# A cached attention block: warm-up matmuls of 80 columns, branch hints moved forward, the last product in two halves

## The chip, the core and the metric

The kernel runs on one core of a Trainium2 chip. The metric is the device time of one execution in microseconds. A profile is one further execution, recorded by the hardware profiler; its times count from the first instruction of the program.

## The reference

```python
B, Sq, D = 8, 112, 640
H, Sk, Dh = 32, 512, 192
q = (x @ wq).reshape(B, Sq, H, Dh).transpose(0, 2, 1, 3)
scores = einsum("bhqd,bhkd->bhqk", q, k_cache) * (Dh ** -0.5)
p = softmax(scores, axis=-1)
o = einsum("bhqk,bhkd->bhqd", p, v_cache)
return o.transpose(0, 2, 1, 3).reshape(B, Sq, H * Dh) @ wo
```

All tensors are bf16. The caches hold 8 x 32 x 512 x 192 elements each, some 50 MB, and are read once.

## The kernel before

`build_main` does the work. A second program, `build_mha_kernel`, stands behind it in the same instruction stream and runs only if a flag is raised: `build_main` counts softmax sums out of a safe range, and if there are none, every engine jumps over the second program to the end.

The work is cut into 64 units, `NU = 64`; a unit is four heads of one batch element, and eight units of the same heads make a group (`NG = 8`). Of a unit TensorE computes the scores (`do_S`, line 922, 96 matmuls on 32-row tiles), the product with V (`do_PV`, line 943, 16 matmuls) and the transposes of its result (`do_T`, line 954). Between these lie slots, (i, 0) and (i, 1) for step i, which a table fills with "pairs" (`do_pair`, lines 846 and 903): a `Q` pair is one 128-column slice of the next group's query product, an `O` pair one 128-row block of the output product with `wo`. Each pair has two halves, h = 0 and 1, in two PSUM banks, 6 and 7. `bank_free` makes a half wait until the bank's former content has been copied out.

`held` (line 846) is a matmul without a weight load of its own: it uses the weights that are in the array. In a pair, step q loads the weights once by `pe.matmul` for h = 0 and uses them again by `held` for h = 1.

The other engines: VectorE transposes K (`do_KT`, line 1080), reduces the softmax sums (`do_NM`), and copies the halves of an `O` pair out (`do_OE`, line 1104), adding the sum so far. ScalarE computes the exponentials (line 1021) and copies query slices and transposes. GpSimd reorders `wq` and the middle heads of V and keeps the count for the flag. SP issues every DMA in one fixed list (`loads`, line 1285; per unit four pieces of K and four of V, with a wait for the buffer to be free) and then the seven stores of the output (line 1288), each after VectorE's two copies of that block.

**Start.** TensorE first waits for the identity matrix, then runs the warm-up at lines 958 to 962: one matmul of the identity with 240 columns and `WARM = 30` further `held` ones, all into PSUM bank 7, results unused. Then come the transposes of the first four blocks of x (`do_X`, line 842, five per block; a block waits for its piece of x), and the query product of group 0 for the first half of the rows (`do_Q0(c, 0)`, line 869, 120 matmuls on 32-column tiles, four at a time). It waits for the copies of the transposes by VectorE (line 1109) and ScalarE (line 997) and for five pieces of `wq`. The last three blocks of x, the scores of unit 0 and the second half of the query product follow.

**End.** Slot (65, 1) holds the last `O` pair, group 7, block 6. Its two halves are copied out by VectorE and stored by SP.

**Jump.** `get_flag` (line 830) loads the flag into a register of each engine; behind the block's own barrier every engine runs a compare-and-branch (line 1309) to `main_end`. `mark_branch_hint_location` puts a branch-prefetch hint for that jump into an engine's stream at the place where it is called: for TensorE at i = 65 (line 978), ScalarE at the end of i = 64 (1066), VectorE after its loop (1138), GpSimd after unit 63 (1211), SP before the last store (1290).

Of the kernel before, what the change touches and what calls it, by code (L numbers as in the profile page):

```python
# [666 lines left out]
def build_main(nc, x, k_cache, v_cache, wq, wo, out, flag, regs, hints):  # L667
# [4 lines left out]
    NU = NG * B  # L672
    DC = D // 128
    R = B * SQ
    MT = R // 128
# [7 lines left out]
    RW = DH + 2  # L683
    FULL, FRONT, BACK = range(3)
    FILL = {(24, 0): 5, (24, 1): 6, (48, 0): 4, (48, 1): 5, **{(i, j): 2 for i in range(56, 64) for j in range(2)}}
    WARM = 30
    NM = 2
    KP = [4] * NU
# [67 lines left out]
    with ExitStack() as es:  # L756
        def sb(name, shape, dt):
            return es.enter_context(nc.sbuf_tensor(name, shape, dt))
# [27 lines left out]
        ident = sb("ident", [128, 128], BF16)  # L786
        dmy = sb("dmy", [128, 2], F32)
        ps = es.enter_context(nc.psum_tensor("ps", [128, 8, 512], F32))
# [46 lines left out]
        def _(pe):  # L835
# [37 lines left out]
            def do_pair(i, j):  # L873
                if slot[i, j] is None:
                    return
                (k, g, c), part = slot[i, j]
                pair = (k, g, c)
                if k == "Q":
                    if c == 0:
                        W(pe, gW, DC * g)  # L880
                    n, width, inc = DC, HQ, pQ
                else:
                    if part != BACK and 8 * g + last_unit(c) + 1 > min(i - 2 + j, NU - 2):
                        W(pe, aT, 8 * g + last_unit(c) + 1)
                    n, width, inc = 6, HO, pO
                steps = {FULL: range(n), FRONT: range(n // 2), BACK: range(n // 2, n)}[part]
                fill = FILL.get((i, j), 1)
                for q in steps:
                    if k == "Q":
                        w = wqs[:, g % 2, q, 128 * c:128 * (c + 1)]  # L890
                        rhs = [xT[:, q, HQ * h:HQ * (h + 1)] for h in range(2)]
                    else:
                        if c == 0 and q % 2 == 0:
                            W(pe, mWO[g % 2][q // 2], 32 * (g // 2 + 1))
                        w = oT[:, q, 128 * c:128 * (c + 1)]
                        rhs = [wos[:, g % 2, q, HO * h:HO * (h + 1)] for h in range(2)]
                    for h in range(2):
                        if q == 0:
                            bank_free(pe, pair, h)
                        cuts = fill if q else 1  # L900
                        for f in range(cuts):
                            cs = slice(width * f // cuts, width * (f + 1) // cuts)
                            mm = (held if h or f else pe.matmul)(ps[:, 6 + h, cs], w, rhs[h][:, cs], q == 0,  # L903
                                                                 q == n - 1 and f == cuts - 1)
                        if q == n - 1:
                            mm.then_inc(inc, 1)

# [48 lines left out]

            W(pe, gI, 1)
            W(pe, vI, 1)
            warm = ident[:, None, 0:60].broadcast_to([128, 4, 60])
            pe.matmul(ps[:, 7, 0:240], ident[:], warm, start=True, stop=True)  # L960
            for j in range(WARM):
                held(ps[:, 7, 0:240], ident[:], warm, True, True)
            for m in range(4):
                do_X(m)
            for c in range(6):
# [24 lines left out]
        @block.scalar  # L990
        def _(act):
            W(act, vI, 1)
            act.activation(dmy[:, 1:2], dmy[:, 0:1], ACTF.Exp)

            def evac_x(m):
                W(act, pXT, m + 1)
                act.activation(xT[:, :, 128 * m:128 * (m + 1)],
                               psb[:, m, 0:D].rearrange("p (c s) -> p c s", c=DC), ACTF.Copy).then_inc(aX, 1)

            def evac(g, c, h):  # L1000
                n = q_index[g, c, h]
                W(act, pQ, n + 1)
                if g >= 2 and c == 0 and h == 0:
                    W(act, pS, 4 * B * (g - 1))
                act.activation(qT[g % 2][:, c, HQ * h:HQ * (h + 1)], ps[:, 6 + (n % 2 if g == 0 else h), 0:HQ],  # L1005
                               ACTF.Copy).then_inc(aQ, 1)

            def evac_pair(i, j):
                if slot[i, j] and slot[i, j][0][0] == "Q" and slot[i, j][1] != FRONT:
                    for h in range(2):  # L1010
                        evac(*slot[i, j][0][1:], h)

            def exp(u, a):
                W(act, pS, 4 * u + a + 1)
                if a == 3 and u >= 2:
                    W(act, gM, u + 1)
                if a == 0:
                    W(act, pPV, u - 1)
                    if u < 2:
                        W(act, gV, 1)  # L1020
                act.activation(pT[u % 2][:, a, :, 0:SQ], ps[:, a, 0:4 * SQ].rearrange("p (t q) -> p t q", t=4), ACTF.Exp,  # L1021
                               scale=scale).then_inc(aEX, 1)

            def norm(u):
                W(act, vRC, u + 1)
                W(act, pT_, u - 1)
                for e in range(2):
                    ins = act.activation(os_[u % 2][:, DH * (2 + e):DH * (3 + e)], pv_of(u)[0:SQ, 1, e, 1:1 + DH], ACTF.Copy,  # L1028
                                         scale=rinv[:, u % 4, 2 + e:3 + e])
                ins.then_inc(aNM, 1)  # L1030

            def tevac(u):
                g, b = divmod(u, B)
                W(act, pT_, u + 1)
                if g > 0:
                    W(act, pO, 2 * (MT * (g - 1) + (SQ * b + SQ - 1) // 128 + 1))
                src = psb[:, bank_of_T(u), 2:2 + 4 * RW].rearrange("p (k w) -> p k w", k=2)[:, :, 0:3 * SQ]
                act.activation(oT[:, :, SQ * b:SQ * (b + 1)].rearrange("p (k c) q -> p k c q", k=2),  # L1038
                               src.rearrange("p k (c q) -> p k c q", c=3), ACTF.Copy).then_inc(aT, 1)

            for m in (1, 3):
                evac_x(m)
            for c in range(6):
                evac(0, c, 0)
            for m in (4, 5):
                evac_x(m)
            for c in range(6):
                if c < 4:
                    exp(0, c)
                evac(0, c, 1)  # L1050
            for i in range(1, NU + 2):
                if i < NU:
                    exp(i, 0)
                if i >= 2:
                    tevac(i - 2)
                if i < NU:
                    exp(i, 1)
                evac_pair(i, 0)
                if i < NU:
                    exp(i, 2)  # L1060
                    exp(i, 3)
                if 1 <= i <= NU:
                    norm(i - 1)
                evac_pair(i, 1)
                if i == NU:
                    hints[mybir.EngineType.Activation] = act.mark_branch_hint_location()
            get_flag(act)

        @block.vector
        def _(dve):  # L1070
# [52 lines left out]
                        do_OE(*slot[i, j][0][1:], h)  # L1123

            for i in range(NU + 1):
                kts = [divmod(n, 4) for n in range(*kt_ahead[i])]
                for it in kts[:3]:
                    do_KT(*it)
                if i < NU:
                    do_OEs(i, 0)  # L1130
                if i >= 1:
                    do_NM(i - 1)
                if i == NU:
                    do_OEs(i, 0)
                do_OEs(i, 1)
                for it in kts[3:]:
                    do_KT(*it)
            hints[mybir.EngineType.DVE] = dve.mark_branch_hint_location()
            W(dve, gC, NU + 1)
            dve.tensor_reduce(tot[:], cnt[:], axis=mybir.AxisListType.XY, op=ALU.add).then_inc(vT, 1)  # L1140
            W(dve, vT, 1)
# [8 lines left out]
        def _(gp):  # L1150
# [48 lines left out]
            for u in range(NU):  # L1199
# [7 lines left out]
                gp.wait_ge(gC, u + 2)  # L1207
                if u + NM < NU:
                    middle(u + NM)
                if u == NU - 1:  # L1210
                    hints[mybir.EngineType.Pool] = gp.mark_branch_hint_location()
            get_flag(gp)

# [1 line left out]
        def _(sp):  # L1215
            loads = []
# [52 lines left out]
            for u in range(4, NU + 1):  # L1269
# [8 lines left out]
                for g in range(1, NG):  # L1278
                    d = u - (8 * g - 1)
                    if 0 <= d < 3:  # L1280
                        load_wo(g, d)
            for dst, src, s, count, waits in loads:
                for ws, wv in waits:
                    W(sp, ws, wv)
                sp.dma_start(dst, src).then_inc(s, 16)
            for m in range(MT):
                W(sp, vO, 2 * (MT * (NG - 1) + m + 1))
                sp.dma_start(out.rearrange("b s d -> (b s) d")[128 * m:128 * (m + 1)], ob[:, m, :]).then_inc(mOUT[m], 16)
                if m == MT - 2:
                    hints[mybir.EngineType.SP] = sp.mark_branch_hint_location()  # L1290
            get_flag(sp)
            for m in range(MT):
                sp.wait_ge(mOUT[m], 16)
# [49 lines left out]
```

## Time and profile before

| | us |
|---|---|
| five timed runs, median | 406.02 |
| lowest and highest of them | 405.08, 407.72 |
| profiled execution, its own time | 404.48 |
| its span, first to last instruction | 399.4 |
| TensorE busy in the span | 390.8 |
| DMA queue busy, share of 16 engines | 90.2% |
| HBM read over the span | 117.54 MB |

The page gives busy time of each engine, the chain of work that ended last (followed back from the last instruction), and groups of like instructions: line, engine, operation, output and input, count, busy time, mean duration, and what ended the idle time before them. A timeline lists instructions in order of time, merged where they are alike: start, duration of the whole group, engine, line. Matmul ends are modelled, so matmuls in a row overlap: the distance of their starts tells what one costs. The span begins and ends with the program's own instructions; the execution's time is longer by what the runtime does before and after them, instruction fetches among it. Those fetches are DMA packets on two queues of the kind "instruction", q8 and q14.

### The profile page before, as it was taken

The numbers are of one execution on the slowest core, as the hardware profiler recorded it, in microseconds if no ns is written. First come the engines' busy times: TensorE is split into PE (matmuls) and PEld (weight loads), VectorE is DVE, ScalarE is ACT, GpSimd is POOL, SyncE is SP. The second block draws the span as 40 slices with busy tenths as digits, with TensorE's granted clock in tenths as the row PEclk, the third lists the DMA queues.
The fourth block names the chain that finished last, engine by engine and source line by source line (L and its number), as shares of the span: only waits on it lengthen the run. The fifth ranks groups of instructions, "written<-read, shape, count | busy, mean of one in ns | idle before, by whom it ended". The sixth has DMA issues, their size and how long they took to land.

```text
span 399.4 us, 20206 instructions
## 1 busy us (share of the span) xinstructions
PE 390.8 (98%) x9073; PEld 242.4 (61%) x8285; DVE 292.9 (73%) x569; ACT 254.3 (64%) x550; POOL 141.3 (35%) x420
## 2 busy tenths in 40 slices
PE   7999999999999999999999999999999999999995
PEld 1656665656656656565666656666565665667661
DVE  1665788786796787876787776886788677789843
ACT  2577665667656766667756676566764766666661
POOL 5522443243442253233352255233344223223320
PEclk9999999999999999999999999999999999999999
DMA  8999999999998999989998999989899979999611
GB/s 271 375 372 341 328 344 336 350 353 332 368 321 268 308 294 344 316 273 317 319 334 288 286 311 337 337 270 311 260 300 321 316 254 324 302 327 300 208 44 59
DMA packets 88443, 120.04 MB, mean 301 GB/s; under 512 B 9760, under 2 KB 88352, under 8 KB 88352
## 3 DMA queue, kind: packets, MB, share of 16 engines
q1 hardware_dynamic: 88352, 118.72, 90.2%
q8 instruction: 69, 1.13, 1.2%
q14 instruction: 22, 0.18, 0.2%
HBM read 117.54 MB, written 1.15 MB: 297 GB/s over the span
## 4 chain that ended last, share of the span: by engine, by line
PE 96%; DVE 2%; issue 1%; DVEq 0%; POOL 0%; POOLq 0%
PE ps L846 24%; PE ps L943 22%; PE ps L922 21%; PE ps L903 20%; PE ps L954 6%; PE ps L869 1%; PE ps L862 1%; DVE kt L1080 1%; DVE xs L1104 0%; PE ps L842 0%; DVE xT L1109 0%; DVE acc L1104 0%; DVEq L830 0%; PE ps L960 0%; POOL ident L1153 0%
## 5 line engine op out<-in xcount | busy, mean ns | idle before, releaser
L1080 DVE STREAM_TRANSPOSE kt<-kr 128x384 int32<-128x384 int32 x256 | 191.5, 866 | 2.4 <-DMA kr<-in_k_cache_dram 2.1
L1021 ACT ACTIVATE pT<-ps 128x448 bf16<-128x448 f32 x256 | 130.4, 560 | 75.6 <-PE ps L922 75.4
L922 PEld LDWEIGHTS ps<-qT,kt 32*128 32x128 bf16 x6144 | 77.3, 93 | 31.0 <-issue 24.3
L943 PE MATMUL ps<-vs,pT 128*128 128x193 bf16 x512 | 95.2, 247 | 0.1
L846 PE MATMUL ps<-wos,oT 128*128 128x320 bf16 (+3 forms) x476 | 93.8, 267 | 0.0
L1203 POOL TENSOR_SCALAR bad<-rinv 112x4 f32<-112x4 f32 x64 | 14.7, 229 | 220.6 <-DVE rinv L1089 220.6
L903 PE MATMUL ps<-wos,oT 128*128 128x320 bf16 x336 | 90.6, 289 | 0.7 <-DVE xs L1104 0.7
L922 PE MATMUL ps<-qT,kt 32*128 32x112 bf16 x6144 | 88.6, 208 | 1.0 <-issue 0.8
L943 PE MATMUL ps<-vm,pT 128*128 128x193 bf16 x512 | 85.1, 247 | 0.3 <-issue 0.3
L846 PE MATMUL ps<-xT,wqs 128*128 128x448 bf16 (+4 forms) x282 | 74.5, 309 | 0.0
L903 PE MATMUL ps<-xT,wqs 128*128 128x448 bf16 (+2 forms) x210 | 72.8, 347 | 0.2 <-DVE acc L1104 0.2
L1028 ACT ACTIVATE os<-ps,rinv 112x192 bf16<-112x192 f32 x128 | 46.9, 417 | 36.2 <-DVE rinv L1089 34.7
L1185 POOL COPY vm<-vs 128x384 int32<-128x384 int32 x128 | 61.4, 510 | 10.6 <-DMA vs<-in_v_cache_dram 3.8
L903 PEld LDWEIGHTS ps<-wos,oT 128*128 128x128 bf16 x336 | 32.7, 97 | 45.5 <-issue 39.7
L943 PEld LDWEIGHTS ps<-vs,pT 128*128 128x128 bf16 x512 | 47.7, 98 | 18.4 <-ACT oT L1038 10.5
L1005 ACT ACTIVATE qT<-ps 128x448 bf16<-128x448 f32 x96 | 48.0, 552 | 16.8 <-PE ps L903 10.8
L1086 DVE TENSOR_REDUCE sm<-ps 112x4 f32<-112x8 f32 x64 | 10.6, 166 | 57.2 <-PE ps L943 57.0
L1104 DVE TENSOR_TENSOR acc<-ps,acc 128x320 f32<-128x320 f32 x84 | 37.0, 481 | 16.5 <-PE ps L903 16.5
L943 PEld LDWEIGHTS ps<-vm,pT 128*128 128x128 bf16 x512 | 46.6, 97 | 3.0 <-issue 0.2
L1038 ACT ACTIVATE oT<-ps 128x672 bf16<-128x672 bf16 x64 | 46.4, 725 | 1.9 <-PE ps L954 1.9
L903 PEld LDWEIGHTS ps<-xT,wqs 128*128 128x128 bf16 x210 | 20.4, 97 | 35.0 <-issue 30.2
L1092 DVE TENSOR_TENSOR os<-ps,rinv 112x384 bf16<-112x384 f32 x64 | 35.7, 558 | 6.5
(42 smaller groups left out, 177.1 us busy)
## 6 DMA issues: line engine op xcount, KB each, us to landing
kr<-in_k_cache_dram SPq DMA_DIRECT2D x256, 192.0 KB, 4.1
vs<-in_v_cache_dram SPq DMA_DIRECT2D x256, 192.0 KB, 4.0
wos<-in_wo_dram SPq DMA_DIRECT2D x48, 160.0 KB, 4.3
wqr<-in_wq_dram SPq DMA_DIRECT2D x35, 192.0 KB, 5.1
out_dram<-xs SPq DMA_DIRECT2D x7, 160.0 KB, 2.5
wqs<-in_wq_dram SPq DMA_DIRECT2D x5, 192.0 KB, 4.2
xs<-in_x_dram SPq DMA_DIRECT2D x2, 320.0 KB, 3.3
xs<-in_x_dram SPq DMA_DIRECT2D x1, 480.0 KB, 5.7
```

The costliest lines, as they stand in the source:

```text
L846: return pe.add_instruction(mybir.InstMatmult(name=nc.get_next_instruction_name(), engine=mybir.EngineType.PE, ins=[pe.lower_ap_or_imm(rhs ...
L903: mm = (held if h or f else pe.matmul)(ps[:, 6 + h, cs], w, rhs[h][:, cs], q == 0, q == n - 1 and f == cuts - 1)
L922: mm = pe.matmul(ps[:, a, SQ * t:SQ * (t + 1)], kt[u % NT][p, t, c // 2, :, c % 2], qT[g % 2][p, c, SQ * b:SQ * (b + 1)], start=(c == 0), ...
L943: mm = pe.matmul(pv[:, k, e, o0:o0 + DH + 1], pT[u % 2][:, a, t, :], src[:, a, v0:v0 + DH + 1], start=(t == 0), stop=(t == 3), skip_group_ ...
L1005: act.activation(qT[g % 2][:, c, HQ * h:HQ * (h + 1)], ps[:, 6 + (n % 2 if g == 0 else h), 0:HQ], ACTF.Copy).then_inc(aQ, 1)
L1021: act.activation(pT[u % 2][:, a, :, 0:SQ], ps[:, a, 0:4 * SQ].rearrange("p (t q) -> p t q", t=4), ACTF.Exp, scale=scale).then_inc(aEX, 1)
L1028: ins = act.activation(os_[u % 2][:, DH * (2 + e):DH * (3 + e)], pv_of(u)[0:SQ, 1, e, 1:1 + DH], ACTF.Copy, scale=rinv[:, u % 4, 2 + e:3 + e])
L1038: act.activation(oT[:, :, SQ * b:SQ * (b + 1)].rearrange("p (k c) q -> p k c q", k=2), src.rearrange("p k (c q) -> p k c q", c=3), ACTF.Co ...
L1080: dve.transpose(dst, src).then_inc(vKT, 1)
L1092: dve.tensor_tensor(os_[u % 2][:, 0:2 * DH].rearrange("p (e d) -> p e d", e=2), pv[0:SQ, 0, :, 1:1 + DH], rinv[:, u % 4, 0:2][:, :, None]. ...
L1104: ins = dve.tensor_tensor(ob[:, m, cs] if g == NG - 1 else acc[:, m, cs], src, acc[:, m, cs], op=ALU.add)
L1185: ins = gp.tensor_copy(vm[u % NM][:, :, (DH + 2) * h:(DH + 2) * h + DH].bitcast(I32), vs[u % NV][:, :, 32 + DH * (1 + h):32 + DH * (2 + h) ...
```

## The change

Three edits.

1. The warm-up matmuls have 80 columns in place of 240; their number is the same.
2. The hints of four engines stand earlier: ScalarE's at the head of i = 55, VectorE's at the head of i = 60, GpSimd's after unit 53, SP's 56 loads ahead of the end of its list. TensorE's stays.
3. In the pair of slot (65, 1) all six steps of half 0 come first, then all six of half 1, which loads its weights anew at each step. Other pairs are unchanged.

```diff
+    HINT_AT = {"act": 55, "dve": 60, "pool": 53, "sp": 56}
...
-                for q in steps:
+                apart = (i, j) == (NU + 1, 1)
+                for q, hs in [(q, [h]) for h in range(2) for q in steps] if apart else [(q, range(2)) for q in steps]:
...
-                    for h in range(2):
+                    for h in hs:
...
-                            mm = (held if h or f else pe.matmul)(ps[:, 6 + h, cs], w, rhs[h][:, cs], q == 0,
-                                                                 q == n - 1 and f == cuts - 1)
+                            mm = (pe.matmul if h == hs[0] and f == 0 else held)(ps[:, 6 + h, cs], w, rhs[h][:, cs], q == 0,
+                                                                               q == n - 1 and f == cuts - 1)
...
-            warm = ident[:, None, 0:60].broadcast_to([128, 4, 60])
-            pe.matmul(ps[:, 7, 0:240], ident[:], warm, start=True, stop=True)
+            warm = ident[:, None, 0:20].broadcast_to([128, 4, 20])
+            pe.matmul(ps[:, 7, 0:80], ident[:], warm, start=True, stop=True)
             for j in range(WARM):
-                held(ps[:, 7, 0:240], ident[:], warm, True, True)
+                held(ps[:, 7, 0:80], ident[:], warm, True, True)
...
             for i in range(1, NU + 2):
+                if i == HINT_AT["act"]:
+                    hints[mybir.EngineType.Activation] = act.mark_branch_hint_location()
...
-                if i == NU:
-                    hints[mybir.EngineType.Activation] = act.mark_branch_hint_location()
...
             for i in range(NU + 1):
+                if i == HINT_AT["dve"]:
+                    hints[mybir.EngineType.DVE] = dve.mark_branch_hint_location()
...
-            hints[mybir.EngineType.DVE] = dve.mark_branch_hint_location()
...
-                if u == NU - 1:
+                if u == HINT_AT["pool"]:
                     hints[mybir.EngineType.Pool] = gp.mark_branch_hint_location()
...
-            for dst, src, s, count, waits in loads:
+            for n, (dst, src, s, count, waits) in enumerate(loads):
+                if n == len(loads) - HINT_AT["sp"]:
+                    hints[mybir.EngineType.SP] = sp.mark_branch_hint_location()
...
-                if m == MT - 2:
-                    hints[mybir.EngineType.SP] = sp.mark_branch_hint_location()
```

## The prediction

> **What bounds the kernel now.** I read the totals and the chain first, then the start and the end in order of time, then what lies behind the span. From the page:
>
> ```profile
> span 399.4 us, 20206 instructions
> PE 390.8 (98%) x9073; PEld 242.4 (61%) x8285; DVE 292.9 (73%) x569; ACT 254.3 (64%) x550; POOL 141.3 (35%) x420
> PE 96%; DVE 2%; issue 1%; DVEq 0%; POOL 0%; POOLq 0%
> ```
>
> TensorE is busy 98% of the span and is 96% of the chain: from its first real work on, one unit follows another without a hole. So the time is the moment at which TensorE starts real work, plus a stream that the diff doesn't touch, plus what follows its last matmul. The start (timeline):
>
> ```profile
> 1.70 6.10 PE L846 MATMUL ps<-ident 128*128 128x240 bf16 x30
> 7.64 1.28 PE L842 MATMUL ps<-ident,xs 128*128 128x128 bf16 x20
> 8.40 1.30 ACT L997 ACTIVATE xT<-ps 128x640 bf16<-128x640 bf16 x2 [6.17 <-PE ps L842]
> 9.80 5.86 PE L869 MATMUL ps<-xT,wqs 128*32 128x448 bf16 x120 [0.88 <-DVE xT L1109]
> ```
>
> The warm-up takes 6.10/30 = 203 ns per 240 columns, half speed; the trace's clock record grants full speed at 7.56 us, just before the first transpose. The data had been there for long (view of the tile xs, time to landing):
>
> ```profile
> DMA to landing us min/median/max: 3.1/3.5/5.7
> ```
>
> The pieces of x are issued at 0.74, 1.24 and 6.04 us and land at 3.83, 4.70 and 11.76. So TensorE computes nothing useful for 3.8 us after x is there. The end (timeline):
>
> ```profile
> 393.60 0.30 PE L903 MATMUL ps<-wos,oT 128*128 128x320 bf16 x1 [0.45 <-DVE xs L1104]
> 395.26 0.30 PE L846 MATMUL ps<-wos,oT 128*128 128x320 bf16 x1
> 395.46 0.89 DVE L1104 TENSOR_TENSOR xs<-ps,acc 128x320 bf16<-128x320 f32 x2 [1.56 <-PE ps L903]
> ```
>
> Both halves of the last product end together at about 395.4, and VectorE then needs 0.89 for the two. The last store is issued at 396.38. Behind the span, the jumps and the instruction fetches (view of line 1309, then DMA queues from 399.5 to 400.5):
>
> ```profile
> L1309 ACTq COMPARE_BRANCH  x1: 68/68/68, 398.8 to 398.8; - x1
> L1309 PEldq COMPARE_BRANCH  x1: 490/490/490, 398.9 to 398.9; - x1
> ```
> ```profile
> q14 instruction: 4, 0.03, 11.0%
> q8 instruction: 1, 0.02, 9.0%
> ```
>
> Four packets of 8192 B start at 399.78 to 399.92, about 0.9 us after four engines jumped. TensorE's 16384 B follow at 400.18. A semaphore that the program doesn't use rises at 399.73, next only at 402.31 and 403.15, then six times by 403.44; some 200 others are reset until 404.0. I read it as the engines' closing barrier: one engine arrives at once, the others are late. The profiled execution took 404.48 us, its span 399.4, so 5.1 lie outside, most of them here. The timed runs' median is 406.02, 1.54 above this execution; I work out a difference on the profile and add it to the median.
>
> [...]
>
> **The change part by part.** *Warm-up* (31 matmuls, 80 columns for 240). At half speed 80 columns take 203 x 80/240 = 68 ns, the whole 2.1 us from 1.53, ending at about 3.7, before x lands at 3.83. The transposes then start at about 3.9 instead of 7.64. They are still at half speed: 20 x 203 x 128/240 = 108 ns make 2.2 us, to 6.1. ScalarE's second copy (0.65 each, 1.30 for two) follows the last of them with some 0.25 of latency and ends at 7.0, so the query product (L869) starts at about 7.1 instead of 9.80; its first weights landed at 5.89, its fifth piece at 7.94, just about when wanted. The early start thus brings 2.7.[...] The product has 30 steps of 195 ns (5.86/30), double when cold, say 373 to 390[...]. I take 0.9[...]; ends -0.8 and +2.5. What is late next: the third piece of x lands at 11.76, the key transposes end at 13.16, V of unit 0 lands at 19.58 and is wanted at 25.73 less the gain. None bites, so the gain runs through to the end; loads later wait for buffers and move with TensorE.
>
> *Last product.* The same 12 matmuls of 135 ns; the second half loads its six weights again (98 ns each, beside the matmuls, as in the value product, where every matmul has its load). The first half ends near 394.6 and its copy (0.49) lies beside the second half, which no longer waits at 393.9 for its bank and ends at about 395.4. One copy follows: 395.9 instead of 396.35. Gain 0.45, ends 0.2 (loads don't hide) and 0.6. The store, its landing 1.8 us later and the jump follow unchanged.
>
> *Hints.* One instruction per engine moves, 45 to 56 ns each, on engines that have idle time in every unit: nothing. Moved past by SP's hint are 56 load issues; it holds none of them back. What may change is the fetch behind the jump. I counted each engine's instructions in the trace against the 8192 B fetches. ScalarE fetches at its instructions 67, 192, 323, 453, 575, 705 (347.65 us)[...] and jumps at 806. VectorE's last entry is 834 (388.14), jump 857; GpSimd's 454 (356.26), jump 502; SP's 595 (366.52), jump 620. The old hints stand at 798, 841, 497 and 611[...]. From 388.2 to the jump no such packet runs, so these hints fetch nothing. The new ones stand at 697, 790, 439 and 549[...]. The trace doesn't show such a hint at work on these four engines. But somebody reached the barrier at 399.73 without a fetch; only TensorE can have, whose hint at 388.40 is followed by an extra 16384 B at 392.08. If all arrive as early, the barrier is through at about 399.73 + 0.4 = 400.1 or 400.2 instead of 403.44: gain 3.2. Ends 0 (the hint does nothing, or one engine still comes last) and 3.4 (all of 402.31 to 403.15 and the wait before).
>
> Sum: -0.9 - 0.45 - 3.2 = -4.6. On the profiled 404.48 that is 399.9, on the median 406.02 - 4.6 = 401.4.
>
> **The rivals.** *Hints without effect*: [...]one engine misses. Then only start and tail count: -1.35, 404.7; with one of the two late arrivals left (402.31), 0.8 more, 403.9. For it: four hints were useless before.[...] *Clock late*: hints work, the start loses 0.8: -2.9, 403.1.[...] *Slower*:[...] Each engine then stalls at its page entry for a miss, 402.31 - 398.92 = 3.4 us, and misses at the jump as before. GpSimd and SP work units ahead and hide it. ScalarE at 347.7 has 75.6/64 = 1.2 us of idle time per unit before its exponentials, so some 2 stay; VectorE at 388.1 stands in the tail with TensorE behind it, some 2.5. That is +4.5 - 1.35 = +3.1, 409.1; it decides once the stalls exceed 3.4 us. Against it: no old hint fetched at once.
>
> **How the numbers follow.** This kernel's measurement can tell about 0.5%, 2.03 us, from no change: faster is below 404.0, slower above 408.1. All hints work and the clock comes in time: 0.66, 401.4, its own range 399.5 (start +2.5, end +3.4) to 403.2. Clock late: 0.06. Hints without or with partial effect: 0.20, of which 0.04 falls below 404.0 and 0.01 on the far side.[...] Faster 0.66 + 0.06 + 0.04 = 0.76; same 0.15; slower 0.09. The range reaches from 399.4 to 404.7, which takes in the middle of the second case and leaves out some 0.2.
>
> **What would show it.** Warm-up over at 3.7, first transpose at 3.9, query product from 7.1 and ending before 15.66 by about 0.9. The last VectorE line as two copies of 0.49 some 0.8 apart, the last store issued about 0.65 after the last matmul's start, not 1.12. No 8192 B packet within 1.2 us of the jumps, those packets instead at 347, 356, 366 and 388 as before; the gap between time and span down from 5.1 to about 1.9. If that gap stays at 5, the hint step is wrong; if ScalarE or VectorE stand still for 3 us at those page entries, the slower rival is right.

## The result, and the profile after

| | before | after |
|---|---|---|
| timed runs, median, us | 406.24 (48 runs) | 403.32 (27 runs) |
| lowest and highest | 403.93, 410.15 | 400.11, 406.40 |
| ratio of after to before | | 0.992, 95% interval 0.9903 to 0.9937 |
| profiled execution, its own time | 404.48 | 401.15 |
| its span | 399.4 | 399.2 |
| outside the span | 5.1 | 1.9 |

The change is faster by 0.8%, about 3.2 us (the medians differ by 2.9). The ratio and the comparisons below leave out two executions that lay over 1.5% above the fastest of their kernel, one of the change (406.40) and one of the kernel before in the runs of e1 to e4 (411.12). Almost nothing of the gain lies in the span. In the page of the changed kernel the totals, the chain and VectorE's costliest group read:

```profile
span 399.2 us, 20213 instructions
PE 89%; DMA 4%; DVE 4%; issue 1%; SPq 1%; DVEq 0%
L1082 DVE STREAM_TRANSPOSE kt<-kr 128x384 int32<-128x384 int32 x256 | 191.7, 867 | 6.5 <-DMA kr<-in_k_cache_dram 6.1
```

TensorE's share of the chain falls from 96% to 89%, and DMA, which was not in it, has 4%. VectorE's K transposes now wait 6.1 us for K's loads; it was 2.1, in the page before:

```profile
L1080 DVE STREAM_TRANSPOSE kt<-kr 128x384 int32<-128x384 int32 x256 | 191.5, 866 | 2.4 <-DMA kr<-in_k_cache_dram 2.1
```

This is the first sign of where the earlier start went.

**The start.** Timeline of the changed kernel (start, duration of the group, engine, line):

```profile
1.58 2.20 PE L847 MATMUL ps<-ident 128*128 128x80 bf16 x30
...
4.30 2.08 PE L843 MATMUL ps<-ident,xs 128*128 128x128 bf16 x20 [0.52 <-DMA xs<-in_x_dram]
...
7.27 1.80 PE L870 MATMUL ps<-xT,wqs 128*32 128x448 bf16 x16 [0.89 <-DMA wqs<-in_wq_dram]
...
9.23 6.79 PE L870 MATMUL ps<-xT,wqs 128*32 128x448 bf16 x104 [0.15 <-DMA wqs<-in_wq_dram]
```

The warm-up ends at 3.78. The first transpose now waits for x (0.52 us), which in this execution landed at 4.26, and the query product waits for each of its weight pieces, which landed at 7.13 to 9.19, 1.2 us later than in the profile before. The clock record is full from 6.00, half again from 9.41 to 12.82, then full. The stretch from 6.00 to 9.41 holds the hole before the product and its waits for weights: the profile has TensorE busy for 2.05 of these 3.41 us. The product ends at 16.01, against 15.66 before.

**The end.** Timeline of the changed kernel:

```profile
393.85 1.79 PE L905 MATMUL ps<-wos,oT 128*128 128x320 bf16 x12 [0.44 <-DVE xs L1106]
...
394.87 0.49 DVE L1106 TENSOR_TENSOR xs<-ps,acc 128x320 bf16<-128x320 f32 x1 [0.71 <-PE ps L905]
395.68 0.49 DVE L1106 TENSOR_TENSOR xs<-ps,acc 128x320 bf16<-128x320 f32 x1 [0.32 <-PE ps L905]
```

The two copies of the last product stand 0.81 apart, the first beside the matmuls of the second half. From the product's first matmul to the end of the last copy it takes 2.32 us; it was 2.75.

**Behind the span.** DMA queues of the changed kernel from 398.6 on:

```profile
q14 instruction: 4, 0.03, 1.8%
q8 instruction: 1, 0.02, 1.0%
```

The jumps stand at 398.64 to 398.75. Four fetches of 8192 B follow at 399.73 to 399.89; before there were four at 399.78 to 399.92 and three more at 402.76 to 403.48. The semaphore that the program doesn't use, which before rose at 399.73, 402.31 and 403.15, now rises nine times between 399.50 and 399.97. So the four remaining fetches hold nobody up. What they bring isn't shown: the trace tells times and sizes of the packets, not their addresses.

### The profile page after: what moved, and what is told of

Same layout as the page of the kernel before. It is cut to its first block, busy times and chain, and to the rows that moved or that the text cites. A ratio compares the mean times of both kernels' runs of the same rounds, so it can differ in the third digit from the quotient of the medians.

```text
span 399.2 us, 20213 instructions
## 1 busy us (share of the span) xinstructions
PE 389.6 (98%) x9073; PEld 243.6 (61%) x8291; DVE 293.3 (73%) x569; ACT 254.3 (64%) x550; POOL 141.3 (35%) x420
## 4 chain that ended last, share of the span: by engine, by line
PE 89%; DMA 4%; DVE 4%; issue 1%; SPq 1%; DVEq 0%
PE ps L847 21%; PE ps L945 20%; PE ps L905 19%; PE ps L924 19%; PE ps L956 6%; DMA kr<-in_k_cache_dram 2%; DVE kt L1082 2%; PE ps L870 2%; PE ps L863 1%; DMA wqs<-in_wq_dram 1%; SPq L1290 1%; DVE acc L1106 0%; DVE xs L1106 0%; PE ps L843 0%; DVE acc L1103 0%
## 5 line engine op out<-in xcount | busy, mean ns | idle before, releaser
L847 PE MATMUL ps<-wos,oT 128*128 128x320 bf16 (+3 forms) x470 | 92.1, 267 | 0.4 <-issue 0.3
L924 PE MATMUL ps<-qT,kt 32*128 32x112 bf16 x6144 | 87.4, 208 | 0.0
```

The costliest lines, as they stand in the source:

```text
L847: return pe.add_instruction(mybir.InstMatmult(name=nc.get_next_instruction_name(), engine=mybir.EngineType.PE, ins=[pe.lower_ap_or_imm(rhs ...
L924: mm = pe.matmul(ps[:, a, SQ * t:SQ * (t + 1)], kt[u % NT][p, t, c // 2, :, c % 2], qT[g % 2][p, c, SQ * b:SQ * (b + 1)], start=(c == 0), ...
```

## The experiments

Each group of runs stands beside runs of the kernel before on the same chip, so "before" has another median in each: 407.31 for e1 to e4, 406.2 for e5 to e8, 405.56 for e9 to e12. Each execution's time and span are known, so two things are compared: the time outside the span, and the span.

**e1 to e4: the parts alone.** e1 moves the hints and leaves the rest, e2 shortens the warm-up only, e3 divides the last product only, and e4 is the change without the warm-up edit:

```diff
-            warm = ident[:, None, 0:20].broadcast_to([128, 4, 20])
-            pe.matmul(ps[:, 7, 0:80], ident[:], warm, start=True, stop=True)
+            warm = ident[:, None, 0:60].broadcast_to([128, 4, 60])
+            pe.matmul(ps[:, 7, 0:240], ident[:], warm, start=True, stop=True)
```

> Only the four hints moved; warm-up of 240 columns and last product as before. Theory A (the hints give all they were priced at, the shorter warm-up costs on average): about 3.3 us less than before, all of it behind the span, closing barrier through about 0.9 us after the jumps[...]; span as before. Theory B (the warm-up gives its 0.9, but moving the hints disturbs the stream by some 1.6 us): only about 1.7 us less, span 1.6 longer.

> Only the warm-up shortened to 80 columns. Theory A: 0.5 to 1 us slower than before; the clock record falls back to half speed[...] in a part of the executions, which then take about 1.5 us more, the others about nothing less, since the product's weights land no earlier. Theory B: about 0.9 us faster.

> Only the last product in two halves one behind the other. Both theories: about 0.45 us less, in the distance from the first matmul of that product to the end of VectorE's last copy (2.75 before, 2.3 here).

> The change without its warm-up edit: hints and last product, warm-up of 240 columns. Theory A: about 3.75 us less than before, thus 0.5 to 1 better than the change itself (median 403.3 there), and no return of the clock to half speed. Theory B: about 2.2 less, worse than the change.

| | runs | ratio to before (interval) | outside the span, median | mean span and its standard error |
|---|---|---|---|---|
| before | 34 | | 5.37 | 401.8 ± 0.2 |
| e1 hints | 6 | 0.9881 (0.9837 to 0.9926) | 1.81 | 400.7 ± 0.4 |
| e2 warm-up | 14 | 0.9996 (0.9965 to 1.0026) | 5.46 | 401.5 ± 0.4 |
| e3 last product | 22 | 0.9982 (0.9959 to 1.0004) | 5.29 | 401.1 ± 0.3 |
| e4 hints, last product | 6 | 0.9886 (0.9838 to 0.9934) | 1.77 | 401.0 ± 0.6 |

The hints do what theory A says: 3.6 us outside the span (5.37 to 1.81), and in every execution: 1.7 to 2.0 with the hints moved, 4.5 or more without. (The mean span of e1 is shorter too, by 1.1 ± 0.4, which the hints don't explain; in e9 and e10 the span is that of before.) The last product shows its 0.45 in the trace of e3 (first matmul 393.62, end of the last copy 395.93: 2.31); as a ratio it can't be told from nothing. The warm-up is the surprise: neither 0.9 faster (B) nor 0.5 to 1 slower (A) shows; the interval, some 1.4 us faster to 1.1 slower, excludes neither by itself. Of A's clock there is a part: 2 of the 14 executions have a mean clock of 0.996 or less, and spans of 404.0 in the mean against 401.1. The profile of e2 has exactly the early start that was hoped for. Its timeline:

```profile
3.88 2.31 PE L842 MATMUL ps<-ident,xs 128*128 128x128 bf16 x20
...
7.04 6.03 PE L869 MATMUL ps<-xT,wqs 128*32 128x448 bf16 x120 [0.84 <-ACT xT L997]
```

The clock was full from 6.15 and stayed so; the product ended at 13.07 and the scores of unit 0 began at 13.94, where before they began at 16.53: a lead of 2.6. At unit 4 the lead was 1.7 us (39.27 against 40.95); the 0.9 went in two holes of TensorE, 0.91 at 15.66 and 0.50 at 28.20, against one of 0.55 before (the last section has all such holes). At unit 8 the lead was gone: 64.25 against 63.66. Timeline of e2 between them:

```profile
61.04 0.85 DVE L1080 STREAM_TRANSPOSE kt<-kr 128x384 int32<-128x384 int32 x1 [1.87 <-DMA kr<-in_k_cache_dram]
...
61.76 0.85 DVE L1101 COPY acc<-ps 128x320 f32<-128x320 f32 x2
...
62.28 0.31 PE L903 MATMUL ps<-wos,oT 128*128 128x320 bf16 x1 [1.33 <-DVE acc L1101]
```

VectorE waits 1.87 us for a piece of K; behind it in its order stands the copy of an output half; TensorE needs that half's bank and stands still for 1.33. The pair before it, at 55.66, was held up in the same way by less. These two places make 2.22 of the 2.29 us that e2 lost between units 4 and 8, at full clock. The profile before has no such gap there:

```profile
59.66 1.64 DVE L1080 STREAM_TRANSPOSE kt<-kr 128x384 int32<-128x384 int32 x2
...
61.16 0.86 DVE L1101 COPY acc<-ps 128x320 f32<-128x320 f32 x2
...
61.91 0.30 PE L903 MATMUL ps<-wos,oT 128*128 128x320 bf16 x1
```

And K landed no earlier: that of units 8 and 9 at 54.38 and 61.02 in e2, at 54.25 and 60.40 before, where TensorE was 1.7 us behind. Stages of the kernel before (each row: stretch, its length, busy time of the engines, granted clock, DMA share, GB/s):

```profile
20.00:60.00 40.00, 40.00 (x922) 24.85 (x874) 27.82 (x51) 29.10 (x64) 14.43 (x42) 1.00 1.02 346
60.00:110.00 50.00, 49.97 (x1113) 31.35 (x1036) 39.42 (x77) 32.95 (x73) 17.87 (x51) 1.00 1.02 348
110.00:208.00 98.00, 97.40 (x2333) 60.38 (x2107) 75.51 (x146) 63.05 (x138) 36.54 (x106) 1.00 0.95 309
208.00:390.00 182.00, 181.55 (x4404) 116.46 (x3998) 139.96 (x276) 120.07 (x263) 61.28 (x183) 1.00 0.88 283
```

Up to 110 us the DMA share is at 1.02, later at 0.95 and 0.88, though TensorE is busy all the time. That gave a new theory, D: the loads set the pace up to about 62 us, and an earlier start only meets them earlier. D names the DMA engines as what limits the loads. The trace leaves room for another limit, SP, which issues them one by one. Timeline of e2, SP alone:

```profile
53.83 2.58 SPq L1285 DMA_DIRECT2D kr<-in_k_cache_dram  x4
56.45 1.85 SPq L1285 DMA_DIRECT2D vs<-in_v_cache_dram  x4
58.35 0.91 SPq L1285 DMA_DIRECT2D wos<-in_wo_dram  x2
59.30 2.84 SPq L1285 DMA_DIRECT2D kr<-in_k_cache_dram  x4
```

SP has no pause there. From 20 to 60 us it issues 69 loads, one each 0.475 us where nothing holds it, which makes 33 of the 40 us; nearly all the rest are eight issues that take 1.0 to 1.6 us in place of 0.43. Seven of them are of K, and they aren't waits for a buffer: each buffer had been free for over 5 us. Whether the DMA engines, SP's issuing or both limit the loads is open.

**e5 and e6: where a hint must stand.** One number each, on top of e4. Theory A here: the hint must stand ahead of its engine's last 8192 B fetch before the jump ("last entry" in the prediction), and not ahead of the one before it. ScalarE's last two are at its instructions 575 and 705 in the profile before, at 579 and 706 (288.81 and 348.04 us) in that of the change, its jump at 806.

```diff
-    HINT_AT = {"act": 55, "dve": 60, "pool": 53, "sp": 56}
+    HINT_AT = {"act": 57, "dve": 60, "pool": 53, "sp": 56}
```

> As e4 (hints, last product, long warm-up), but ScalarE's hint at i = 57: its instruction 719, which is past 706[...], yet 87 instructions ahead of the jump. Theory A[...]: ScalarE misses at the jump, one 8192 B packet more about 0.9 us after the jumps, the closing barrier waits for it; the time outside the span rises from 1.8 to between 4.4 and 5.4 us, nearly all that the four hints gained. Theory C (a hint needs only some distance or time): stays at 1.8.

> As e4, but ScalarE's hint at i = 42, its instruction 531[...]. Theory A:[...] ScalarE either stands still for about 3 us[...] (about 348 us), or misses at the jump and the time outside the span is 4.4 to 5.4 us. Theory C: no stall, outside stays at 1.8.

e5 and e6 are one execution each; the step that they look for, some 3 us outside the span, is far above the scatter of that time (1.7 to 2.0 with the hints of the change). e5, with ScalarE's hint at its instruction 719 (354.6 us), took 404.57 with a span of 399.7: 4.87 outside, against 1.8. After the jumps the same semaphore rose at 399.93 and then only at 403.13. Between 403 and 404 there is one fetch that e4 doesn't have:

```profile
q14 instruction: 1, 0.01, 2.7%
```

So one engine of four costs 3.1 of the 3.6 us, and the time goes with the hint's place against the last fetch, not with the distance: 87 instructions and 44 us ahead of the jump, but 13 behind the fetch, were too late for ScalarE, while VectorE's hint in the change, some 70 instructions and 30 us ahead (368.72, jump at 398.70), stands ahead of its fetch (388.40) and is in time. e6, with the hint at 531 (266.8 us), lost nothing: 1.83 outside, and ScalarE had no hole at 348 beyond the 1.33 us that it idles there before, too. The part of theory A that says that too early is wrong as well fell: this hint stood ahead of both fetches.

**e7 and e8: fewer loads.** Both leave out half of K's bytes for units 3 to 9, e7 on e4, e8 on the change; scores of these units are computed from what the buffer held. With the bytes go 14 of SP's issues, so these runs don't tell SP from the DMA engines.

```diff
-    KP = [4] * NU
+    KP = [2 if 3 <= u < 10 else 4 for u in range(NU)]
...
-                    cs = slice(16 // KP[u] * DH * h, 16 // KP[u] * DH * (h + 1))
+                    cs = slice(4 * DH * h, 4 * DH * (h + 1))
```

> As e4 with the warm-up of 240 columns, but for units 3 to 9 only half of K's bytes are loaded (the other half is what the buffer held), which takes some 2.7 MB out of the loads of the first 60 us. Theory D (the early start is lost because the DMA engines are saturated up to about 62 us, where VectorE waits for K and TensorE for VectorE): scores of unit 8 start where TensorE alone would be, about 63 us or a little before, without a stall near 62. Theory E (it is lost by the clock alone): same as e4, no difference to it beyond noise.

> As e7 with the warm-up of 80 columns (the change itself, half of K left out for units 3 to 9). Theory D: the lead at the start, 1 to 2.5 us where the clock doesn't fall back, is still there at unit 8 (scores at 61 to 62 us against 63) and the span is about 1 us shorter than e7's. Theory E: no shorter than e7, some executions longer.

Start of the scores of a unit, in the profiles (us):

| | unit 4 | unit 8 | from 4 to 8 |
|---|---|---|---|
| e9, the change again | 38.79 | 64.17 | 25.38 |
| e2, short warm-up | 39.27 | 64.25 | 24.98 |
| e6 | 39.63 | 63.67 | 24.04 |
| e4 | 39.94 | 64.57 | 24.63 |
| e3 | 40.23 | 63.62 | 23.39 |
| e1 | 40.43 | 63.80 | 23.37 |
| after | 40.47 | 63.81 | 23.34 |
| e10, e4 again | 40.71 | 64.40 | 23.69 |
| before | 40.95 | 63.66 | 22.71 |
| e5 | 41.03 | 63.94 | 22.91 |
| e7, half K | 41.47 | 64.16 | 22.69 |
| e8, half K, short warm-up | 39.29 | 61.98 | 22.69 |

With all of K, unit 8 begins at 63.6 to 64.6, wherever unit 4 began: who comes 2 us earlier stands 2 us longer. With half of K, four units take 22.69 us in both, which is what TensorE needs. The cleanest pair is e2 and e8: unit 4 at 39.27 and 39.29, unit 8 at 64.25 and 61.98. That is theory D as far as it says "the loads"; theory E, the clock alone, is out for e2 and e9, which have full clock from 6.15 and 5.86 to the end of the span. (e7 missed the "about 63" of its expectation because it reached unit 4 late, not by a stall.) Against e7, e8 leads by 2.2 at unit 8 and by 1.6 at the end (unit 63 at 380.51 against 382.15). In the timed runs the difference can't be told from nothing: mean span 398.3 ± 0.5 for e8 and 398.9 ± 0.5 for e7, four runs each. The start differs from execution to execution, by landing times and by the clock, which in e8's profile is full only from 10.94.

**e9 to e12: the pair once more, and an attempt to mend it.** e9 is the change and e10 is e4 again. e11 and e12 put VectorE's K transposes of steps 0 to 11 behind its copies, so that a late K holds up nobody else, and let the scores of units below 15 wait for them:

```diff
+                late = i < 12
-                for it in kts[:3]:
+                for it in [] if late else kts[:3]:
                     do_KT(*it)
...
-                for it in kts[3:]:
+                for it in kts if late else kts[3:]:
                     do_KT(*it)
```

> The change once more, beside e10 on the same chip. Theory D (the DMA engines set the pace up to about 62 us): the same as e10 within the interval, ratio to before about 0.990; scores of unit 8 start at 63.6 to 64.6 us, wherever those of unit 4 stood. Theory E (the clock's fall back alone): 0.5 to 1 us slower than e10.

> e4 once more, beside e9. Theory D: same as e9 within the interval, ratio to before about 0.990. Theory E: 0.5 to 1 us faster than e9.

> The change with VectorE's K transposes of steps 0 to 11 put behind its copies and normalisations of the step (and a wait on them ahead of each of these units' scores). Theory D: VectorE's wait for K at about 61 us no longer holds up the copy that TensorE waits for; the stall near 62 goes, scores of unit 8 start 0.5 to 2 us before 63.6, and some of it is left at the end, about 1 us less than e9. If TensorE then waits for K itself, or VectorE's later transposes come last, it is no faster than e9 or slower.

> As e11 with the warm-up of 240 columns. Theory D: 0.5 to 1 us slower than e11, about as e10 or 0.5 faster, since it starts later and meets the same loads. Theory E: no slower than e11.

| | runs | ratio to before (interval) | mean span |
|---|---|---|---|
| before | 19 | | 400.1 ± 0.3 |
| e9 | 6 | 0.991 (0.988 to 0.994) | 399.9 ± 0.4 |
| e10 | 14 | 0.9921 (0.9897 to 0.9945) | 400.4 ± 0.4 |
| e11 | 6 | 1.0477 (1.0441 to 1.0513) | 422.7 ± 0.6 |
| e12 | 6 | 1.0447 (1.0413 to 1.0481) | 421.7 ± 0.5 |

e9 and e10 are the same within their intervals, as D expects; a difference of 0.9 is within them as well. e11 and e12 miss by far, in the way that the expectation of e11 named last: the transposes come last themselves. And D expected e12 to be slower than e11, which it isn't. Waits of e11 from 20 to 80 us (who waited for whom, total, times, longest):

```profile
PE ps L924 <- DVE kt L1082: 13.2, 7, 2.5
```

TensorE waits for them seven times there, some 2 us each time, and in this profile the clock falls to half for 3.41 us three times, at 36.72, 53.78 and 77.68. Their place at the head of each step was worth more than the wait that it causes. No version here beats the change.

## Why the prediction was right, and which term was mis-sized

The forecast was 401.4, 4.6 less than the median; measured was 2.9 less (403.32), with an interval of 2.6 to 3.9 by the ratio. The direction and the main term were right; the term of the warm-up was not.

*Hints, forecast -3.2.* Right, and slightly more: 5.37 to 1.8, so -3.6 over many executions, -3.2 in the two profiles. The reading that decided it was the count of each engine's instructions against its fetches. That a hint ahead of the last fetch would work was the author's estimate; the profile before had TensorE's hint alone for it. The runs show it: 1.8 us outside the span with all four hints there (e1), 4.87 with ScalarE's 13 instructions behind its last fetch (e5), so 3.1 us for one engine. One detail of the forecast was wrong: it expected no fetch within 1.2 us of the jumps, but four of 8192 B still run there (399.73 to 399.89), and the semaphore's last rise is at 399.97 all the same. The rival "hints without effect" is out, and so is the slower one, which stood at 0.08: after their fetches at 348 and 388 ScalarE idles 1.33 us and VectorE 0.75, the same as before, also when ScalarE's hint came one fetch earlier (e6).

*Last product, forecast -0.45.* Right in the traces: 2.75 to 2.32 in the change, 2.31 in e3. The six added weight loads lie beside the matmuls: twelve matmuls start 135 ns apart, as before.

*Warm-up, forecast -0.9.* Mis-sized: no gain can be told from nothing (e2: 0.9996, interval 0.9965 to 1.0026; e9 against e10 the same), and in the traces the lead is gone at unit 8. The start itself went as worked out: transposes at 3.88 and product at 7.04 in e2, against 3.9 and 7.1. The end of the product went with the clock: 13.07 in e2, where it was full from 6.15, and 14.83 in e8, where it was full only from 10.94; before, where it began at 9.80, it was 15.66. When the clock would come, and with it the 0.9 between its ends of -0.8 and +2.5, was the author's estimate, which the profile before doesn't show. What failed is the sentence that followed: "None bites, so the gain runs through to the end; loads later wait for buffers and move with TensorE". I looked at first landings up to V of unit 0 and stopped there. The loads don't move with TensorE before they wait for buffers, and that begins long after 62 us: in e2 the first piece of K that is issued as its buffer comes free is that of unit 15, at 85 us. K of the earlier units comes at the loads' own pace, and unit 8 begins at 63.6 to 64.6 in any case. A part of the lead, 0.9 of 2.6 in e2, went before that, in the holes at 15.66 and 28.20. The page had shown the pace of the loads, in the DMA row of nines and in GB/s of 375 and 372 in the second and third slice, against a mean of 301; I read the row as an average and didn't ask in which stage the loads had no slack.

The rival "clock late" had the number, 403.1, but not the mechanism: in e2 and e9 the clock comes in time and the lead is lost all the same. The clock is a smaller part. In the profile after the record's steps at 6.00, 9.41 and 12.82 are 3.41 apart, and the fall to half at 9.41 follows a stretch in which TensorE was busy for 2.05 of 3.41 us; what makes it fall isn't shown. This fall, which the forecast didn't list, costs that profile its early start: 3.41 us at half clock are 1.7 us of work, by estimate, and the product ends at 16.01. Of 28 executions of the change, the profiled ones among them, 9 had a mean clock of 0.996 or less, with spans of 402.0 in the mean against 400.8 for the others; before, such executions were 3 of 34 beside e1. That this makes part of the gap between the sum (-3.6 - 0.45) and the measured -2.9 is likely but not shown: in e9 none of six had it, and its ratio of 0.991 is inside the first one's interval. The scatter of medians of the kernel before between the groups, 405.56 to 407.31, is larger than what remains. The traces show one thing that scatters as much, TensorE's holes of the last section: from unit 8 to unit 63 the profiles with all of K and the transposes in their old place take 318.1 to 320.8 us, and the holes make 0.3 to 3.2 us of it, 3.2 and 3.1 in the two slowest (e4: 320.76, e10: 320.27) and 0.3 in that of before (318.67).

## What to carry to other kernels

Before an earlier start is booked as a gain, find the first stage in which another stream of work has no slack and ask whether that stream starts earlier too: a lead over loads that already run at their limit is a wait, only later (2.6 us at the start of e2, none at unit 8). One late hint of four cost 3.1 us behind the jump, all four 3.6 (e5, e1), so give every engine its own, ahead of its last fetch before the jump; count instructions against the fetches in the trace to place them. And an engine's wait for a load holds up what stands behind it (VectorE's 1.87 us for K, 1.33 of TensorE, in e2), but moving that work back can cost more: here some 2 us in each of seven units (e11).

## What the runs showed of the hardware

- A hint behind its engine's last 8192 B fetch before the jump cost 3.1 to 3.6 us behind the jump, whether one engine's or four's (e5: 4.87 us outside the span, before: 5.37, none: 1.8). In the span of the profile before 22 fetches are of 8192 B (q14) and 69 of 16384 B (q8). By the count of instructions I put the first down to ScalarE, VectorE, GpSimd and SP (ScalarE's stand 122 to 131 instructions apart) and the second to TensorE.
- ScalarE's hint in e6, at its instruction 531, stood ahead of its last two fetches, 132 us before the jump, and worked: 1.83 us outside the span.
- TensorE stops at times in the middle of a unit, where it has no wait of its own and no semaphore ends the hole. Timeline of e1, and the fetches on TensorE's queue from 137.5 to 138.5:

```profile
140.00 0.26 PE L945 MATMUL ps<-vm,pT 128*128 128x193 bf16 x1 [1.04 <-issue]
```
```profile
q8 instruction: 1, 0.02, 6.8%
```

  Counted in each trace, all 45 such holes over 0.25 us in the fourteen profiles (from 10 to 390 us) stand at the same place of TensorE's instructions, 193 to 195 modulo 256: at 5826 in e1's line above, elsewhere at 449, 963, 6081, 6337, 16065 and so on. Before the end of each a fetch of 16384 B had begun, 2.3 to 3.5 us ahead (at 137.59 here). I read them as waits for that fetch, which no record of the trace names. Why some fetches have such a hole and others not was not tried.
- The same load of the same program lands earlier or later from one execution to the next: the first weight piece at 5.5 to 6.2 us in thirteen profiles and at 7.13 in that of the change.
